# A scanned attention and a feed-forward block on one core: new tables of order, engines, banks and filler products

## The chip, the cores and the metric

The kernel runs on one core of one Trainium2 chip. The metric is the device time of one execution in microseconds. Before the change it is 268.63 us, the median of three runs (267.58 to 268.67).

## The reference

Inputs `r, k, v, w, a, b` are float32 of shape (4, 8, 768, 40): batch, heads, positions, head size. Every head carries a 40 by 40 state through the 768 positions; the rows that it gives are then put through a feed-forward block of 3072 tokens, 320 to 2048 to 320, with a squared ReLU.

```
for t in range(S):
    y[:, :, t] = einsum('bhd,bhde->bhe', rt, state)
    Sa = einsum('bhde,bhe->bhd', state, at)
    state = state * wt[:, :, None, :] - einsum('bhd,bhe->bhde', Sa, bt)
    state = state + einsum('bhd,bhe->bhde', vt, kt)
h = x @ w_in;  r = maximum(h, 0);  out = (r * r) @ w_out
```

## The kernel before, in words

The scan over 768 positions is cut into 6 chunks of 128 positions. A *batch* m (24 of them) is one chunk of one of the four inputs' batches, all 8 heads; a *step* st (48) is half a batch, four heads. Each batch is prepared (`add_prep`), each step goes through the products that solve the recurrence inside a chunk (`add_step`), and when both steps of a batch are done its 128 tokens go into the feed-forward block (`add_ff`, 14 groups h, of one batch for the first four and of two after them).

Preparation of a batch: six loads of 160 KB (`NW`, `NK`, `NB`, `NA`, `NV`, `NR`, L293), all issued from SyncE (SP); the logarithm of w on ScalarE (`lnW`, L307); sums over positions on TensorE (L317, L321, L328) into a bank; exponentials on ScalarE (`GI`, `GA`, L352); a copy of `GA` shifted by one position, `E`, by two small transfers from SP (L362; the first three batches compute it, L332); the products `KB` (L383) and `AA` (L389) and the casts `RV` (L246); then transposes, on TensorE with a copy out of the bank (`AT`, `KBT`, `RVT`, L399 with L243 or L246), or from batch 10, 16 and 20 on by a transposing transfer from SP (L426).

A step: 8 products L522 into two banks, two masked copies on VectorE (`CN`, L530), products `P` (L539, L545), a copy `Mc`, correction L554, difference `c` (L567), correction again, a copy `SN`, a transpose and copy `TB`, 8 products L608, two masked copies on VectorE (`EVX`, L613), products y (L628 to L646), then `Xn` (L652) and `UZ` (L659). `x` (L571) and `Cc` (L575) feed a sum that guards the result.

Feed-forward: transposes of `Xn` (L765) to `XT`, products with the 320 by 2048 weights `WIN` (L790 for the last 64 rows, L803 for the others), ReLU `hs` (L810 on ScalarE, L812 on VectorE), square `Gt` (L819, L821), products with `WOUT` (L837), copy `osb` and a store (L845). `WIN` and `WOUT` are loaded by transfers that GpSimd (POOL) issues (L727, L730, L739).

Nothing here is ordered by a scheduler at run time. Each operation is registered by `op(...)` with the engines that could do it; `placed()` then reads four tables that are written out in the code. `ORDER` is one list of all 2135 operations: each engine executes its own in the order of that list, and waits there for what it needs, with everything behind it on that engine waiting too. `WAYS` picks the engine of the operations that have a choice (VectorE, ScalarE, GpSimd). `BANKS` picks one of the eight accumulator banks for each group of products. `IDLE` puts so many products of ones, whose result nobody reads (L1010), ahead of a TensorE operation. A bank, or a buffer of a ring, that is still in use holds up its next writer.

Of the kernel before, what the change touches and what calls it, by code (L numbers as in the profile page):

```python
# [18 lines left out]
def kernel(  # L19
# [14 lines left out]
    NB, NHH, T, D = r.shape  # L34
    L = 128
# [227 lines left out]
    for m in range(NBC):  # L263
        o = Batch()
# [613 lines left out]
    def add_guard():  # L878
# [32 lines left out]
        "!,!3#C!!#I!(!&!$!+!6!-#L!7!<!?!=!@!O!8!9!>$@!P!4!F!A!;$F!S!D!*!E!I!V#J#K!W!K!J!L!Q#E!T!U"  # L911
        "!:!R!o!B!Z#M!G!2#D#F!H!q!p$I!#!r$G![!]#Q!M$K#R!^$H!d!_#N#S!X!`%;!N#O%A!a!b!c!Y!s#X$J!5%B"
        "%C$C#G$A#Y$D$B&:)6$E!t!.#T#V#W$L$M#q!u#P#]#_&~!C%D%F!v!w#s#^#r#H!{!|%E!g!}$O$P$N!e!/!f#!"
        "#`%<%=#t$S$U!~$R!h#u#v&@$T&A!i!x#a#b$Q##$V((!y!j&B&C#c#d$Y#w#x!k#%#$#U$[&D#y#e#f$Z$n#(#)"
        "$p#Z%K$]#}!l#[$^#i&E$_!1#.()%I!m#~!%$!#g$o#&!n%L#z#j$#$`$$(*%J#k#l#/#0$W#1%H%>$w$X$c&H$q"
        "$r%R%G$s$a!z#{&I$%&<#h%S$&&G&;&=)<#5$t#2#3#8$u$+#m$v#6%M#n#<$z#o$(!0$b&F%?%P$f%Q#|$x(!#4"
        "$d#=%@$,$-#7(+$e&J%k(#$g&K$y&>!)#p)z&L$.(&${#9(%%m#:%l)=%t#;%V%X$|$h%W&?$i(,%N$/&Q$2$~$}"
        ")>(-%Y$0&O%n&R%!%Z%O%[(0$j%#%%$k%T%]$l$m%$($%o&P(.(/%p%`%q(1$1%U)?&U%r%s%^$5%w&V&W)@#>%x"
        "$3%_(3(2%u&M(9%&(:)A&j$4&N%(%a&k&l%y%c$6)D&X&m$9%z(6$7*#(5%d&n+2+v&s$:$8&_)E%{%e%)&Y&o%*"
        "(4%-(7&p%g%+&q&r&Z#,#*%f*$#+%.+8(8%|&S&T&v%~&[%}(=(>(?*%#-(;&])8(Q(S%v%0%4%h(<&^%b*&&w(@"  # L920
        "&t+9&u)7&x)9)B)C):(A%j(R%i)|);*(*)(F(T(B$;$<&`(C(D*,&a&z){*-%1&b(U(V)G&$(G&c+|(E(H#?(Z%2"
        "&d(W(X(I&!&y+:([&e(J)}&{&|(h*++4(Y#@)F&f&%-.&#**&&(K#A&g(^(L(M(_)M)H&h&i%,+;+=+<+}+5)~)K"
# [12 lines left out]
        "10/C11+*/V0%2x/W)1/o.=1.2{1$++/X*b.>121m+,/p1/2z/`,l.?,t,{,x.Q,u/@.R.S,y,s/A.9,|,}/Y/E.@"
# [42 lines left out]
    IDLE = ((132, 1, 1), (38, 21, 4), (60, 4, 5), (135, 2, 5), (62, 1, 5), (223, 11, 7), (168, 1, 5), (89, 3, 4), (230, 11, 7), (232, 6, 6), (239, 5, 7), (241, 2, 5), (109, 1, 0))  # L978
# [140 lines left out]
```

## Time and profile before

| | before |
|---|---|
| span of the profiled execution | 267.4 us |
| runs | 268.67, 267.58, 268.63 us |
| TensorE busy (matmul) | 247.5 us, 93% |
| VectorE (DVE) busy | 236.8 us, 89% |
| ScalarE (ACT) busy | 205.0 us, 77% |
| GpSimd (POOL) busy | 176.7 us, 66% |
| HBM | 123 GB/s over the span |

The profile has no time of its own for the execution beside the span of 267.4 us from the first to the last instruction; the median of the runs is 1.2 us above that span. Busy TensorE time is not TensorE at its peak, since matmuls overlap and their ends are modelled.

### The profile page before, as it was taken

The numbers are of one execution on the slowest core, as the hardware profiler recorded it, in microseconds if no ns is written. First come the engines' busy times: TensorE is split into PE (matmuls) and PEld (weight loads), VectorE is DVE, ScalarE is ACT, GpSimd is POOL, SyncE is SP. The second block draws the span as 40 slices with busy tenths as digits, with TensorE's granted clock in tenths as the row PEclk, the third lists the DMA queues.
The fourth block names the chain that finished last, engine by engine and source line by source line (L and its number), as shares of the span: only waits on it lengthen the run. The fifth ranks groups of instructions, "written<-read, shape, count | busy, mean of one in ns | idle before, by whom it ended". The sixth has DMA issues, their size and how long they took to land.

```text
span 267.4 us, 10182 instructions
## 1 busy us (share of the span) xinstructions
PE 247.5 (93%) x3972; PEld 194.3 (73%) x3972; DVE 236.8 (89%) x559; ACT 205.0 (77%) x549; POOL 176.7 (66%) x289
## 2 busy tenths in 40 slices
PE   7888599999999999999989999999999998799993
PEld 6566487777788687778768688777777786577772
DVE  4799969998999989999999998998999997787681
ACT  3577659897668999687888879898969898477640
POOL 3559559769749999975684747974865754356220
PEclk9999979999999999999999999999999999999998
DMA  7999989899899579899897389997898888771202
GB/s 125 186 166 150 208 164 161 148 175 170 161 171 167 109 137 205 125 166 175 169 190 141 83 165 177 162 150 156 168 165 159 160 171 164 155 182 21 75 2 77
DMA packets 184553, 39.86 MB, mean 149 GB/s; under 512 B 176331, under 2 KB 184118, under 8 KB 184502
## 3 DMA queue, kind: packets, MB, share of 16 engines
q1 hardware_dynamic: 181942, 36.56, 76.6%
q0 software_dynamic: 2560, 2.62, 6.1%
q8 instruction: 31, 0.51, 0.8%
q14 instruction: 20, 0.16, 0.2%
HBM read 28.84 MB, written 3.93 MB: 123 GB/s over the span
## 4 chain that ended last, share of the span: by engine, by line
PE 50%; DMA 14%; DVE 14%; SPq 7%; ACT 5%; POOL 5%; issue 4%; DVEq 0%; POOLq 0%; ACTq 0%
PE bank L837 14%; PE bank L803 10%; SPq L293 6%; DVE CN L530 4%; PE bank L790 4%; DVE EVX L613 3%; DMA WOUT<-in_moe_w_out_dram 3%; PE bank L522 3%; DMA WIN<-in_moe_w_in_dram 3%; PE bank L608 3%; PE bank L399 3%; PE bank L554 3%; PE bank L628 2%; DMA KBT<-KB 2%; PE bank L321 2%
## 5 line engine op out<-in xcount | busy, mean ns | idle before, releaser
L613 DVE TENSOR_TENSOR EVX<-bank,MEX 128x512 bf16<-128x512 f32 x96 | 62.6, 682 | 2.4 <-PE bank L608 1.4
L530 DVE TENSOR_TENSOR CN<-bank,MCN 128x512 bf16<-128x512 f32 x96 | 61.7, 680 | 3.4 <-PE bank L522 2.9
L837 PE MATMUL bank<-WOUT,Gt 128*128 128x320 bf16 x384 | 59.1, 299 | 1.6 <-DMA WOUT<-in_moe_w_out_dram 0.5
L803 PE MATMUL bank<-XT,WIN 128*128 128x256 bf16 (+1 forms) x448 | 55.0, 258 | 0.0
L810 ACT ACTIVATE hs<-bank 128x512 bf16<-128x512 f32 x74 | 43.0, 598 | 12.1 <-PE bank L803 5.5
L837 PEld LDWEIGHTS <-Gt 128*128 128x128 bf16 x384 | 35.2, 97 | 14.6 <-issue 1.6
L821 POOL TENSOR_TENSOR Gt<-hs 128x512 bf16<-128x512 bf16 x35 | 36.2, 1042 | 14.1 <-DVE hs L812 12.1
L803 PEld LDWEIGHTS <-WIN 128*128 128x128 bf16 x448 | 34.7, 98 | 5.5 <-issue 0.6
L579 ACT ACTIVATE junk<-CN 128x512 bf16<-128x512 bf16 x48 | 30.2, 630 | 1.0 <-DVE CN L530 0.5
L571 POOL TENSOR_TENSOR x<-Mc,c 128x160 f32<-128x160 bf16 x40 | 19.9, 502 | 15.0 <-DVE Cc L575 9.1
L819 ACT ACTIVATE Gt<-hs 128x512 bf16<-128x512 bf16 x39 | 24.5, 631 | 5.2 <-DVE hs L812 5.0
L575 POOL TENSOR_TENSOR Cc<-x,SN 128x160 bf16<-128x160 f32 x41 | 21.6, 526 | 3.8 <-ACT SN L243 1.8
L389 POOL TENSOR_TENSOR AA<-NA,E 128x320 bf16<-128x320 f32 (+1 forms) x20 | 15.7, 783 | 12.4 <-DMA E<-GA 6.1
L383 POOL TENSOR_TENSOR KB<-NK,GI 128x320 bf16<-128x320 f32 (+1 forms) x22 | 18.7, 852 | 7.2 <-DMA NK<-in_k_dram 3.6
L554 PEld LDWEIGHTS <-CN 128*128 128x128 bf16 x384 | 18.8, 97 | 6.4 <-issue 3.5
L383 POOL TENSOR_TENSOR KB<-NB,GI 128x320 bf16<-128x320 f32 (+1 forms) x21 | 18.4, 875 | 6.7 <-ACT hs L810 3.4
L335 POOL TENSOR_TENSOR r<-lnW 128x320 f32<-128x320 f32 x18 | 13.1, 728 | 12.3 <-ACT lnW L307 6.2
L243 ACT ACTIVATE TB<-bank 128x512 bf16<-128x512 bf16 (+1 forms) x32 | 17.4, 548 | 4.5 <-PE bank L595 3.2
L522 PE MATMUL bank<-AT,KBT 64*128 64x128 bf16 x384 | 18.5, 217 | 2.1 <-DMA AT<-AA 0.8
L790 PE MATMUL bank<-XT,WIN 64*128 64x256 bf16 (+1 forms) x224 | 18.5, 259 | 1.9 <-DMA WIN<-in_moe_w_in_dram 1.9
L812 DVE TENSOR_SCALAR hs<-bank 128x512 bf16<-128x512 f32 x22 | 14.8, 684 | 4.5 <-PE bank L803 3.4
L608 PE MATMUL bank<-RVT 64*128 64x128 bf16 x192 | 15.3, 219 | 2.3 <-ACT hs L810 1.3
(128 smaller groups left out, 656.8 us busy)
## 6 DMA issues: line engine op xcount, KB each, us to landing
NW<-in_w_dram SPq DMA_DIRECT2D x24, 160.0 KB, 3.6
NK<-in_k_dram SPq DMA_DIRECT2D x24, 160.0 KB, 3.8
NB<-in_b_dram SPq DMA_DIRECT2D x24, 160.0 KB, 3.7
NA<-in_a_dram SPq DMA_DIRECT2D x24, 160.0 KB, 3.9
NR<-in_r_dram SPq DMA_DIRECT2D x24, 160.0 KB, 3.7
NV<-in_v_dram SPq DMA_DIRECT2D x24, 160.0 KB, 3.7
out_dram<-osb SPq DMA_DIRECT2D x24, 160.0 KB, 2.4
E<-GA SPq DMA_DIRECT2D x21, 112.0 KB, 3.3
```

The source lines that it names most:

```text
L383: engine(eng).tensor_tensor(out=o.KB.tile[:, u, h, 0:D], in0=o.nat[key].tile[:, h], op=ALU.mult, in1=o.GI.tile[:, h])
L522: nc.tensor.matmul(out=quads(ca[s])[:, i, u, :], lhsT=o.KBT.tile[half(s), u, j0 + i, :], rhs=o.AT.tile[half(s), j0 + i, :], start=(i == 0 ...
L530: nc.vector.tensor_tensor(out=t_[:, :, s], in0=quads(ca[s]), in1=MCN[:], op=ALU.mult)
L554: nc.tensor.matmul(out=P[:, 2 * i + s], lhsT=CN[:, i, s, 1, :], rhs=X[:, 2 * i + s], start=False, stop=last, skip_group_check=True)
L579: nc.scalar.activation(out=t_, in_=CN_.tile[:, :, :, 1, :], func=ACTF.Square, accum_out=ACC[:, AN + st:AN + st + 1])
L613: nc.vector.tensor_tensor(out=sb(EV_, [128, 2, 2, 2, L], BF16)[:, :, s], in0=quads(ex[s]), op=ALU.mult, in1=MEX[:].rearrange("p (i u) x -> ...
L790: nc.tensor.matmul(out=hv(w_)[:, u], lhsT=WIN[2][half(w_), j * 128:(j + 1) * 128], rhs=XT()[half(w_), 2, 0:nb, :], start=(u == 0), stop=False,
L803: nc.tensor.matmul(out=hv(w_)[:, u], lhsT=WIN[g][:, (j0 + u) * 128:(j0 + u + 1) * 128], rhs=XT()[:, g, 0:nb, :], start=False, stop=(g == 1 ...
L810: nc.scalar.activation(out=t_, in_=hpb.tile[:], func=ACTF.Relu)
L819: nc.scalar.activation(out=t_, in_=x_, func=ACTF.Square)
L821: engine(eng).tensor_tensor(out=t_, in0=x_, in1=x_, op=ALU.mult)
L837: nc.tensor.matmul(out=opb.tile[:, 0:DM], lhsT=Gtb[h].tile[:, j, b_, :], rhs=WOUT[:, j, :], start=(j == 0), stop=(j == NJ - 1))
```

## The change

Only the four tables are new. The operations, their sizes, the tiles, the rings and the loads are the same.

- `ORDER`: nearly every operation stands elsewhere. 
- `WAYS`: 21 operations leave GpSimd; 14 of them go to VectorE and 7 to ScalarE, net. Counted by kind, before to after, on VectorE: `SN` 6 to 21, `x` 8 to 14, `TB` 16 to 22, `Cc` 7 to 12, `AA` 5 to 9, `lo` 1 to 4, `KB` 7 to 9, `AT` 11 to 13; `Mc` 19 to 11, `hs` 22 to 15, copy of `Xn` 12 to 8, `RVT` 10 to 8, `KBT` 7 to 5, casts `RV` 5 to 3, `Gt` 22 to 21, `r` 3 to 2, `XT` 8 to 7, `osb` 10 to 9. On GpSimd: `KB` 43 to 41, `Cc` 41 to 36, `x` 40 to 34, `Gt` 35 to 36, casts 31 to 24, `AA` 20 to 16, `lo` 20 to 17, `r` 18 to 19, copy of `Xn` 12 to 16. On ScalarE: `hs` 74 to 81, casts 14 to 23, `Mc` 29 to 37, `SN` 42 to 27, `TB` 32 to 26, `RVT` 7 to 9, `KBT` 4 to 6, `AT` 10 to 8.
- `BANKS`: another bank for most groups of products.
- `IDLE`: 69 products of ones become 76; before they end ahead of the first feed-forward group, now ahead of step 6's second correction.
- Of TensorE's L837 products, 72 stand behind the last L628 product in the old order, 64 in the new.

```
@@ placed()'s tables; two lines of each long one @@
     ORDER = (
-        "!,!3#C!!#I!(!&!$!+!6!-#L!7!<!?!=!@!O!8!9!>$@!P!4!F!A!;$F!S!D!*!E!I!V#J#K!W!K!J!L!Q#E!T!U"
+        "!6!9!8!3!7!+!4#C!,!!!(!<!5$@!=!?!;!>!F!@!&!#!I!:!%!Q!J!P!T!O!D!U#F!V!E!K!W#I!2#E!o!L!p$F"
...
     WAYS = (
-        "0012201001001111100011001100021202001100011110000110000100100020100001010000001000001100"
+        "0011210111121110111110000100001202000000221110001010010000202020100000201100111010011000"
...
     BANKS = (
-        "0123456725743652745274532031645073610376154731576135372650613724567143726073062173671532"
+        "0123456702345672301427401324713610276732450632046401304620176347201732154603712645135207"
...
-    IDLE = ((132, 1, 1), (38, 21, 4), (60, 4, 5), (135, 2, 5), (62, 1, 5), (223, 11, 7), (168, 1, 5), (89, 3, 4), (230, 11, 7), (232, 6, 6), (239, 5, 7), (241, 2, 5), (109, 1, 0))
+    IDLE = ((26, 5, 6), (38, 9, 6), (49, 7, 0), (51, 4, 0), (82, 6, 4), (89, 19, 2), (148, 13, 3), (155, 6, 6), (349, 4, 1), (331, 6, 3),)
```

The code that reads them, unchanged:

```
        for o, x in zip([o for o in row if o.alts], WAYS, strict=True):
            o.eng, o.cost, o.lat = o.alts[int(x)]
        at = [DIGITS.index(a) * 91 + DIGITS.index(b) for a, b in zip(ORDER[::2], ORDER[1::2], strict=True)]
        for i, n, bank_ in IDLE:
            row[i].idle = n, bank_
```

First place: SyncE at the start of the program, the first loads. `NW_176` before and `NW_165` after are batch 0's w; `NW_167` before and `NW_176` after are batch 1's. Before:

```order
L293 DMA NW_167<-in_w_dram 128x8x40
L293 DMA NW_176<-in_w_dram 128x8x40
L293 DMA NK_181<-in_k_dram 128x8x40
L293 DMA NB_190<-in_b_dram 128x8x40
L293 DMA NA_192<-in_a_dram 128x8x40
L293 DMA NW_195<-in_w_dram 128x8x40
```

After:

```order
L293 DMA NW_165<-in_w_dram 128x8x40
L293 DMA NA_167<-in_a_dram 128x8x40
L293 DMA NB_169<-in_b_dram 128x8x40
L293 DMA NK_172<-in_k_dram 128x8x40
L293 DMA NW_176<-in_w_dram 128x8x40
L293 DMA NW_184<-in_w_dram 128x8x40
```

Batch 0's w moved from second to first, its a from fifth to second; batch 1's w from first to fifth.

Second place: GpSimd around the issue of the first feed-forward weights. Before:

```order
L383 TENSOR_TENSOR KB_91<-NK_368,GI_187 128x8x40
L571 TENSOR_TENSOR x_470<-Mc_313,c_340 128x160
L203 MEMSET SN_110 128x4x24
L575 TENSOR_TENSOR Cc_473<-x_470,SN_107 128x160
L246 CAST RV_104<-NR_378 128x8x40
L571 TENSOR_TENSOR x_561<-Mc_313,c_418 128x160
L339 TENSOR_TENSOR lo_362<-r_360 128x320
L727 DMA WIN_116<-in_moe_w_in_dram 128x2048
L730 DMA WIN_117<-in_moe_w_in_dram 64x1024 x2
L383 TENSOR_TENSOR KB_92<-NK_481,GI_275 128x8x40
L203 MEMSET SN_112 128x4x24
L246 COPY Xn_589<-Xn_589 128x64
```

After:

```order
L383 TENSOR_TENSOR KB_91<-NK_373,GI_197 128x8x40
L383 TENSOR_TENSOR KB_91<-NB_409,GI_197 128x8x40
L730 DMA WIN_117<-in_moe_w_in_dram 64x1024 x2
L246 CAST RV_104<-NV_457 128x8x40
L727 DMA WIN_115<-in_moe_w_in_dram 128x2048
L727 DMA WIN_116<-in_moe_w_in_dram 128x2048
L383 TENSOR_TENSOR KB_92<-NK_502,GI_325 128x8x40
```

The weights stand right behind batch 2's `KB`, where five elementwise operations and a memset stood between; the last piece, `WIN_115`, stood four operations further on and now stands with the others. On TensorE, 353 matmuls stood ahead of the first product that reads `WIN` (L790), and 425 do now.

Third place: VectorE at the last batch's `AA`, which waits for the last `E` transfer. Before:

```order
L530 TENSOR_TENSOR CN_297<-bank_84,MCN 128x2x256
L821 TENSOR_TENSOR Gt_1052<-hs_810 128x512
L613 TENSOR_TENSOR EVX_475<-bank_82,MEX 128x2x256
L389 TENSOR_TENSOR AA_101<-NA_719,E_99 128x8x40
L246 COPY Xn_1013<-Xn_1013 128x64
```

After:

```order
L613 TENSOR_TENSOR EVX_541<-bank_85,MEX 128x2x256
L383 TENSOR_TENSOR KB_92<-NB_487,GI_325 128x8x40
L652 TENSOR_TENSOR Xn_1026<-bank_84,E_96 128x160
L652 TENSOR_TENSOR Xn_567<-bank_81,E_97 128x160
L246 COPY Xn_1026<-Xn_1026 128x64
L567 TENSOR_TENSOR c_341<-bank_82,Mc_1219 128x160
L652 TENSOR_TENSOR Xn_567<-bank_85,E_97 128x160
L389 TENSOR_TENSOR AA_101<-NA_599,E_99 128x8x40
```

`AA` stood between the two `EVX` of one step; now all four `EVX` of the two steps and six smaller operations stand ahead of it.

124 lines of the change are left out of this document (62 added, 62 removed).

## The prediction

> **What bounds the kernel now.** I read the page first, then the program cut in three by what VectorE (DVE) does: before its first `CN`, up to its last `EVX`, and the rest. The columns of a window are its length, then each engine's busy time, granted clock, DMA share, GB/s.
>
> ```profile
> span 267.4 us, 10182 instructions
> PE 247.5 (93%) x3972; PEld 194.3 (73%) x3972; DVE 236.8 (89%) x559; ACT 205.0 (77%) x549; POOL 176.7 (66%) x289
> ...
> 0.00:11.10 11.10, 8.69 (x80) 6.78 (x80) 5.48 (x23) 5.22 (x13) 4.99 (x17) 1.00 0.91 149
> 11.10:247.55 236.45, 223.19 (x3757) 176.17 (x3755) 220.90 (x510) 192.37 (x521) 168.15 (x268) 0.99 0.89 157
> 247.55:267.40 19.85, 15.59 (x146) 11.37 (x142) 10.45 (x28) 7.38 (x16) 3.61 (x6) 0.94 0.14 52
> ```
>
> In the long middle TensorE and VectorE are both near full: VectorE is busy 220.90 of 236.45 us. So the middle cannot shrink by better hops alone. It can shrink only where VectorE idles (236.45 - 220.90 = 15.55 us), where its instructions take longer than they need, or where work leaves it. I therefore make the sum on VectorE: start, middle, tail. Two stretches carry much of the idle time:
>
> ```profile
> 28.00:37.00 9.00, 6.44 (x108) 5.19 (x104) 6.73 (x20) 4.02 (x14) 3.71 (x8) 0.81 0.98 190
> 221.00:233.00 12.00, 9.72 (x147) 7.44 (x144) 8.66 (x20) 7.62 (x19) 4.63 (x9) 1.00 0.79 156
> ```
>
> ```profile
> PE bank L790 <- DMA WIN<-in_moe_w_in_dram: 1.9, 2, 1.5
> DVE AA L389 <- DMA E<-GA: 1.8, 1, 1.8
> PE bank L522 <- DMA AT<-AA: 0.8, 1, 0.8
> ```
>
> VectorE idles 9.00 - 6.73 = 2.27 us in the first and 12.00 - 8.66 = 3.34 us in the second, 5.6 together. The waits (who waited for what: total, times, longest) name the cause: the feed-forward weights land late in the first, the last `E` and a transposed `AA` in the second. All three are transfers that stood too close to their reader.
>
> **Start.** These are ScalarE's and VectorE's rows (start, length, instruction, idle time before and what ended it):
>
> ```profile
> 3.86 0.47 ACT L307 ACTIVATE lnW<-NW 128x320 f32<-128x320 f32 x1 [1.54 <-DMA NW<-in_w_dram]
> 5.09 0.47 ACT L307 ACTIVATE lnW<-NW 128x320 f32<-128x320 f32 x1 [0.76 <-DMA NW<-in_w_dram]
> ...
> 7.55 0.91 DVE L205 MEMSET UZ<- 128x1024 uint32 x1 [0.16 <-issue]
> 8.38 0.26 DVE L389 TENSOR_TENSOR AA<-NA,E 128x160 bf16<-128x160 f32 x1
> ```
>
> Batch 0's logarithm is the second, at 5.09; with its w loaded first it takes the first's place, 1.23 us earlier. The first `AA` stood behind a memset of 0.91 us, which now runs before any load has landed, so up to 2.1 us could be won at the first `CN`. Against it, batch 0's k is now the fourth load and not the third, and a place in the queue is worth about as much as the two logarithms are apart; and what stands on VectorE up to step 3 is more work than before. Ends 0 and -2.1; I take **-1.5 us**, nearer the logarithms' own rows.
>
> **Work that moves to VectorE.** Mean durations are the figure behind "busy us,":
>
> ```profile
> L248 DVE TENSOR_SCALAR SN<-bank 128x160 bf16<-128x160 f32 x6 | 1.8, 319 | 0.3 <-PE bank L554 0.3
> L571 DVE TENSOR_TENSOR x<-Mc,c 128x160 f32<-128x160 bf16 x8 | 4.3, 539 | 0.0
> L246 DVE COPY TB<-bank 128x512 bf16<-128x512 bf16 (+1 forms) x16 | 6.5, 407 | 0.1
> L575 DVE TENSOR_TENSOR Cc<-x,SN 128x160 bf16<-128x160 f32 x7 | 3.3, 473 | 0.0
> L389 DVE TENSOR_TENSOR AA<-NA,E 128x320 bf16<-128x320 f32 (+1 forms) x5 | 2.7, 533 | 1.8 <-DMA E<-GA 1.8
> L339 DVE TENSOR_TENSOR lo<-r 128x320 bf16<-128x320 f32 x1 | 0.7, 731 | 0.0
> ...
> L812 DVE TENSOR_SCALAR hs<-bank 128x512 bf16<-128x512 f32 x22 | 14.8, 684 | 4.5 <-PE bank L803 3.4 <-ACT Gt L819 0.8
> L246 DVE CAST Mc<-bank 128x160 bf16<-128x160 f32 x19 | 5.9, 315 | 0.4 <-PE bank L545 0.4
> L246 DVE COPY Xn<-Xn 128x64 bf16<-128x64 bf16 x12 | 4.3, 362 | 0.1
> L246 DVE COPY RVT<-bank 128x1024 bf16<-128x1024 bf16 (+1 forms) x10 | 6.5, 653 | 0.0
> ```
>
> Added: 15 `SN` 4.8, 6 `x` 3.2, 6 `TB` 2.4, 5 `Cc` 2.4, 4 `AA` 2.1, 3 `lo` 2.2, and 4 of `KB` and `AT` at about `AA`'s 0.53, 2.1: 19.2 us. Removed: 7 `hs` 4.8, 8 `Mc` 2.5, 4 `Xn` copies 1.4, 2 `RVT` 1.3, and eight others (two `KBT`, two casts, one each of `Gt`, `r`, `XT` and `osb`) at 0.56, between these rows, 4.5: 14.5 us. **+4.7 us** of VectorE time. VectorE is busy 93% of the middle, so nothing hides it; I carry it whole. ScalarE gets 7 `hs` and 9 casts for fewer `SN` and `TB`; with 192.37 of 236.45 us busy in the middle it has room, and I cost this at nothing. Were its cover gone, seven operations of about 0.6 us would be 4 us.
>
> **TensorE.**
>
> ```profile
> L1010 PE MATMUL bank<-ones_b 128*128 128x128 bf16 x69 | 6.1, 221 | 0.1
> ```
>
> Seven more products of ones at 6.1/69 = 0.09 us are 0.6 us, and they stand in the first third, where TensorE waits anyway (2.56 us idle in 28 to 37 alone). Nothing on the sum; 0.6 if that cover is gone.
>
> **Idle time recovered.** The sizes and landings of the transfers (KB each, median us to landing):
>
> ```profile
> E<-GA SPq DMA_DIRECT2D x21, 112.0 KB, 3.3
> ...
> WIN<-in_moe_w_in_dram POOLq DMA_DIRECT2D x2, 512.0 KB, 8.0
> ```
>
> ```profile
> L613 DVE TENSOR_TENSOR EVX<-bank,MEX 128x512 bf16<-128x512 f32 x96 | 62.6, 682 | 2.4 <-PE bank L608 1.4 <-ACT junk L714 0.5
> L821 DVE TENSOR_TENSOR Gt<-hs 128x512 bf16<-128x512 bf16 x22 | 12.4, 565 | 0.1
> L571 POOL TENSOR_TENSOR x<-Mc,c 128x160 f32<-128x160 bf16 x40 | 19.9, 502 | 15.0 <-DVE Cc L575 9.1 <-DVE c L567 4.4 <-DVE GL L375 1.3
> ```
>
> The weights move ahead of five GpSimd operations, `x`, `Cc`, a cast, `x` and `lo`, some 2.5 us at the 0.50 of GpSimd's `x` (last row), the last piece by four more, and 72 more matmuls stand ahead of the first reader. Eight microseconds of landing then end before the reader comes: I expect that wait of 1.9 us gone. The last `AA` gets three `EVX` and six small operations ahead of it; the `EVX` alone are 3 x 0.68 = 2.0 us, against the 1.8 us that it waited. Of the 5.6 us in the two holes I take 4.6 back. Of the other 15.55 - 5.6 = 9.9 us, spread over the middle at under 5%, I take 2: counted in `ORDER`, at least 40 TensorE matmuls now stand between the place of any `E` transfer and its first reader, median 108, where ten of the 42 had fewer (two of them none) and the median was 74; for the weights the smallest count goes from 63 to 157. **-6.6 us**; ends 0 (each gap is filled by another late operand) and -12.
>
> **Waits inside VectorE's instructions.** These are minimum, median and maximum durations of single kinds on VectorE:
>
> ```profile
> L571 DVE TENSOR_TENSOR x<-Mc,c x8: 308/460/869, 60.1 to 233.7; 128x160 f32<-128x160 bf16 x8
> L575 DVE TENSOR_TENSOR Cc<-x,SN x7: 310/318/999, 32.5 to 250.1; 128x160 bf16<-128x160 f32 x7
> L821 DVE TENSOR_TENSOR Gt<-hs x22: 411/423/930, 47.5 to 259.6; 128x512 bf16<-128x512 bf16 x22
> L246 DVE COPY Xn<-Xn x12: 171/237/1042, 36.4 to 248.9; 128x64 bf16<-128x64 bf16 x12
> L652 DVE TENSOR_TENSOR Xn<-bank,E x48: 307/315/326, 25.2 to 248.7; 128x160 bf16<-128x160 f32 x48
> ```
>
> The same instruction takes 308 or 869 ns, with no wait outside it. Against the minimum, 8 `x` lose 8 x 0.23 = 1.8, 7 `Cc` 7 x 0.16 = 1.1, 12 copies 12 x 0.19 = 2.3, and 22 `Gt`, whose mean is 565, 22 x 0.15 = 3.4: 8.6 us over 49 instructions, 0.18 each. All of them read and write SBUF alone, as GpSimd's do; the last row, a product that reads a bank, stays between 307 and 326. GpSimd loses 21 operations. If the tables place these instructions where GpSimd is between two of its own, up to 8.6 us could go; if they meet more often, it grows. I take **-2.5 us**, in the lower half because the number of exposed instructions rises. Ends -8.6 and +8.
>
> The Trainium skill, SBUF — State Buffer, section "Who interferes with whom", says that VectorE and GpSimd share one pair of ports as an exclusive lock, also for a two-input VectorE operation with both inputs in SBUF, and that the later one blocks until the other is done. The maxima above agree: 869 is 308 and about one GpSimd operation. By that rule moving work from GpSimd to VectorE buys little where the two run together; a whole block for each of the 20 moved two-input operations is the slower rival below.
>
> **Tail.**
>
> ```profile
> 247.88 1.25 PE L837 MATMUL bank<-WOUT,Gt 128*128 128x320 bf16 x8
> 248.96 0.33 PE L765 MATMUL bank<-IDb,Xn 128*128 128x128 bf16 x3
> ```
>
> Eight L837 products move from behind the last y to ahead of it, where TensorE has gaps. They held TensorE from 247.88 to 248.96: **-1.1 us**. The rest of the tail has the same pieces. End 0, if `Xn` is then late instead.
>
> **Sum.** 267.4 - 1.5 + 4.7 - 6.6 - 2.5 - 1.1 = 260.4 us of span; the median of the runs is 1.2 above the span of before (268.63 against 267.4), which gives **261.6 us**.
>
> **Rivals.**
> 1. *VectorE blocked by GpSimd: slower.* `x`, `Cc`, `AA`, `lo` and `KB` on VectorE rise by 20. If each loses what the worst rows lose (869 - 308 and 999 - 310, about 0.6) and not the 0.2 in its mean, that is 20 x 0.4 = 8 us instead of the 2.5 gained: 260.4 + 10.5 = 270.9 of span, 272.1. It decides against before once the exposed instructions lose 7.0 us more than I take, 0.13 us for each of some 55. For it: the rows above. Against: GpSimd has less to do. 0.13.
> 2. *No change.* The holes close, but VectorE's idle time comes back in front of `CN` and `EVX`: 3 of 15.55 us recovered, no port wait saved: 267.4 - 1.5 + 4.7 - 3.0 - 1.1 = 266.5, 267.7. For it: both engines are near full, so a late operand anywhere costs. 0.13.
> 3. *Twice the gain.* Idle time falls by 12 and port waits by 6: 267.4 - 1.5 + 4.7 - 12 - 6 - 1.1 = 251.5, 252.7. For it: if order and durations agree, VectorE can run at over 98%. Against: no stretch of before does over 10 us. 0.14.
> 4. *The clock halves more often.* In 28 to 37 us the granted clock was 0.81, so about 3.4 us ran at half and 1.7 were lost. The filler products that stood there are gone. Two more such stretches: 261.6 + 3.4 = 265.0. 0.06. The Trainium skill, TensorE: Matmul & The Clock Gate, section "What's actually happening", has the clock halved after an idle window of some 3.4 us; the 0.81 agrees with one such window.
>
> The forecast itself has 0.54, with its own range 257 to 266.
>
> **Chances and range.** A measurement of this kernel can tell about 0.5% from no change, 1.3 us: 267.3 to 270.0. Faster: nearly all of the forecast 0.53, rival 3 0.14, rival 4 0.05, some of rival 2 0.05, 0.77. Slower: rival 1 less its lower end 0.11, a little of rival 2, 0.13. Same: 0.10. The range reaches from 253.5, between rival 3 and the forecast, to 269.5, which leaves out most of rival 1 above and half of rival 3 below.
>
> **What would show it.** Start: the first `CN` on VectorE at 9 to 10 us, not 11.1. Weights: no wait of L790 for `WIN`, and a clock of 1.00 from 25 to 40 us. VectorE: busy over 95% between first `CN` and last `EVX`, and a middle of 229 to 233 us. Port waits: medians of `x` and `Gt` near 310 and 410 ns. Tail: under 19 us after the last `EVX`. The forecast is wrong if VectorE's busy time in the middle grows by over 7 us, or if its idle time there stays above 12 us.

## The result, and the profile after

The changed kernel takes 266.29 us (median of 11 runs, 263.08 to 268.62), the kernel before 268.94 us in the same rounds (11 runs, 267.06 to 271.84). The ratio is 0.987, with a 95% interval of 0.983 to 0.991: 1.3% faster, about 3.5 us where 7 were forecast. The ratio leaves out runs in a slower state (for the changed kernel 4 of 11, the profiled one at 267.04 us among them, by a narrow margin), while the medians of all runs differ by 2.65 us, 1.0%. Two more measurements on other chips gave 0.985 (0.975 to 0.996) and 0.990 (0.985 to 0.994).

The page of the changed kernel, first lines (span, then busy time, share and instructions of each engine):

```profile
span 265.6 us, 10167 instructions
PE 248.5 (94%) x3982; PEld 195.9 (74%) x3982; DVE 233.5 (88%) x573; ACT 207.9 (78%) x556; POOL 163.7 (62%) x268
```

The changed program, cut as in the prediction at VectorE's first `CN` and last `EVX` (length, busy time of TensorE, its weight loads, VectorE, ScalarE, GpSimd, granted clock, DMA share, GB/s):

```profile
0.00:9.85 9.85, 7.98 (x75) 6.56 (x75) 6.57 (x23) 4.49 (x10) 3.78 (x18) 1.00 0.90 147
9.85:247.20 237.35, 225.94 (x3775) 178.70 (x3776) 218.07 (x526) 195.86 (x529) 156.02 (x245) 0.99 0.89 157
247.20:265.60 18.40, 14.54 (x139) 10.62 (x135) 8.84 (x25) 7.54 (x19) 3.86 (x6) 1.00 0.15 56
```

Start and tail came as forecast: 11.10 to 9.85 us and 19.85 to 18.40. The middle did not: 236.45 became 237.35 us. VectorE's busy time there fell by 2.8 us (220.90 to 218.07), and its idle time grew by 3.7 (15.55 to 19.28). What VectorE saved, it waited. Two more profiles of the changed kernel, on other chips (spans 268.8 and 266.2 us), say the same: between their own cuts VectorE is busy for 219.3 and 218.6 us and idle for 21.9 and 19.1.

When it waits is seen in three stretches, of before first and then of the changed kernel (same columns):

```profile
0.00:60.00 60.00, 51.10 (x847) 40.42 (x847) 50.78 (x131) 42.70 (x115) 39.65 (x80) 0.97 0.98 165
60.00:210.00 150.00, 145.73 (x2445) 115.29 (x2446) 144.67 (x335) 126.22 (x344) 113.51 (x175) 1.00 0.91 158
210.00:250.00 40.00, 37.50 (x573) 29.16 (x570) 33.16 (x76) 29.91 (x78) 21.51 (x35) 1.00 0.64 132
```

```profile
0.00:60.00 60.00, 53.62 (x884) 43.63 (x885) 52.51 (x138) 45.45 (x125) 35.65 (x72) 0.94 1.00 167
60.00:210.00 150.00, 146.62 (x2468) 117.11 (x2468) 140.26 (x340) 128.95 (x348) 106.28 (x163) 1.00 0.88 155
210.00:250.00 40.00, 36.49 (x538) 26.69 (x538) 33.18 (x77) 28.64 (x75) 19.70 (x31) 1.00 0.71 142
```

Between 60 and 210 us, where VectorE idled for 5.33 of 150 us, it now idles for 9.74 (10.74 and 10.31 in the other two profiles). In this pair TensorE idles less up to 60 us (8.9 to 6.4) and more from 210 to 250 (2.5 to 3.5). The two holes that the prediction named are mostly closed, and no product waits for `WIN` any more:

```profile
28.00:37.00 9.00, 7.65 (x104) 5.39 (x103) 7.85 (x22) 6.68 (x18) 3.78 (x9) 0.64 0.97 182
221.00:233.00 12.00, 11.78 (x174) 8.42 (x171) 10.70 (x25) 6.92 (x16) 7.77 (x13) 1.00 0.81 152
```

VectorE's idle time in them went from 5.6 to 2.45 us (9.00 - 7.85 and 12.00 - 10.70). Its waits in the changed kernel (who waited for what: total, times, longest):

```profile
DVE CN L530 <- PE bank L522: 3.4, 5, 2.0
DVE hs L812 <- PE bank L803: 3.3, 6, 1.2
DVE c L567 <- PE bank L554: 2.3, 4, 0.8
DVE hs L812 <- POOL Gt L821: 2.1, 2, 1.2
```

Most of it is waiting for TensorE. Summed over VectorE's waits between the cuts, TensorE ended 8.8 us of them before the change and 13.6 after it; transfers ended 1.8 and 0.5. The growth is largest ahead of the difference `c`, less ahead of `CN`, and there is none ahead of `EVX`. Their rows (busy us, mean ns, idle time before them and what ended it), before and then after; the row of `EVX` before stands in the prediction:

```profile
L530 DVE TENSOR_TENSOR CN<-bank,MCN 128x512 bf16<-128x512 f32 x96 | 61.7, 680 | 3.4 <-PE bank L522 2.9 <-ACT GI L352 0.3
L567 DVE TENSOR_TENSOR c<-bank,Mc 128x160 bf16<-128x160 f32 x48 | 15.0, 316 | 0.7 <-POOL RV L246 0.3 <-DVE c L567 0.2
```
```profile
L613 DVE TENSOR_TENSOR EVX<-bank,MEX 128x512 bf16<-128x512 f32 x96 | 62.6, 679 | 2.1 <-PE bank L608 1.5 <-ACT SN L243 0.2
L530 DVE TENSOR_TENSOR CN<-bank,MCN 128x512 bf16<-128x512 f32 x96 | 61.5, 680 | 4.3 <-PE bank L522 3.4 <-ACT junk L579 0.5
L567 DVE TENSOR_TENSOR c<-bank,Mc 128x160 bf16<-128x160 f32 x48 | 14.4, 314 | 3.5 <-PE bank L554 2.3 <-POOL x L571 0.4 <-PE bank L539 0.3
```

TensorE in turn waits late in the program for a transfer that it did not wait for before, the transposed `RVT` (1.2 us in three waits beside its weight loads):

```profile
PE bank L608 <- DMA RVT<-RV: 1.2, 3, 0.5
PE bank L522 <- DMA AT<-AA: 0.7, 1, 0.7
```

### The profile page after: what moved, and what is told of

Read it like the earlier page. It is cut to its first block, busy times and chain, and to the rows that moved or that the text cites. A ratio compares the mean times of both kernels' runs of the same rounds, so it can differ in the third digit from the quotient of the medians.

```text
span 265.6 us, 10167 instructions
## 1 busy us (share of the span) xinstructions
PE 248.5 (94%) x3982; PEld 195.9 (74%) x3982; DVE 233.5 (88%) x573; ACT 207.9 (78%) x556; POOL 163.7 (62%) x268
## 4 chain that ended last, share of the span: by engine, by line
PE 53%; DVE 14%; DMA 11%; ACT 7%; SPq 7%; issue 4%; POOL 2%; DVEq 0%; ACTq 0%
PE bank L837 14%; PE bank L803 10%; SPq L293 5%; DVE CN L530 4%; PE bank L790 3%; DMA RVT<-RV 3%; PE bank L522 3%; PE bank L608 3%; PE bank L399 3%; DVE EVX L613 2%; PE bank L628 2%; PE bank L554 2%; PE bank L321 2%; DMA E<-GA 2%; DMA NW<-in_w_dram 2%
## 5 line engine op out<-in xcount | busy, mean ns | idle before, releaser
L837 PE MATMUL bank<-WOUT,Gt 128*128 128x320 bf16 x384 | 59.0, 299 | 0.7 <-DVE EVX L613 0.6
L810 ACT ACTIVATE hs<-bank 128x512 bf16<-128x512 f32 x81 | 47.0, 599 | 11.9 <-PE bank L803 6.3
L821 POOL TENSOR_TENSOR Gt<-hs 128x512 bf16<-128x512 bf16 x36 | 37.3, 1043 | 27.9 <-ACT hs L810 17.1
L837 PEld LDWEIGHTS <-Gt 128*128 128x128 bf16 x384 | 35.5, 98 | 13.6 <-issue 1.0
L571 POOL TENSOR_TENSOR x<-Mc,c 128x160 f32<-128x160 bf16 x34 | 16.5, 489 | 11.9 <-DVE c L567 8.1
L243 ACT ACTIVATE TB<-bank 128x512 bf16<-128x512 bf16 (+1 forms) x26 | 14.5, 558 | 7.3 <-PE bank L590 2.8
L790 PE MATMUL bank<-XT,WIN 64*128 64x256 bf16 (+1 forms) x224 | 18.7, 259 | 0.7 <-DVE XT L246 0.2
L522 PE MATMUL bank<-AT,KBT 64*128 64x128 bf16 x384 | 17.7, 217 | 1.8 <-DVE KBT L246 0.7
L383 POOL TENSOR_TENSOR KB<-NB,GI 128x320 bf16<-128x320 f32 (+1 forms) x19 | 16.6, 875 | 3.9 <-DMA NB<-in_b_dram 2.2
L628 PE MATMUL bank<-KB,EVX 128*128 128x40 bf16 x384 | 17.4, 181 | 0.9 <-DVE EVX L613 0.9
L575 POOL TENSOR_TENSOR Cc<-x,SN 128x160 bf16<-128x160 f32 x36 | 17.9, 500 | 0.2
L567 DVE TENSOR_TENSOR c<-bank,Mc 128x160 bf16<-128x160 f32 x48 | 14.4, 314 | 3.5 <-PE bank L554 2.3
L628 PEld LDWEIGHTS <-EVX 128*128 128x128 bf16 x384 | 14.7, 97 | 3.7 <-DVE EVX L613 2.5
```

Of the source, the lines that this page charges most:

```text
L383: engine(eng).tensor_tensor(out=o.KB.tile[:, u, h, 0:D], in0=o.nat[key].tile[:, h], op=ALU.mult, in1=o.GI.tile[:, h])
L522: nc.tensor.matmul(out=quads(ca[s])[:, i, u, :], lhsT=o.KBT.tile[half(s), u, j0 + i, :], rhs=o.AT.tile[half(s), j0 + i, :], start=(i == 0 ...
L628: nc.tensor.matmul(out=Y[:, 2 * i + s], lhsT=EV_.tile[:, i, s, u, :], rhs=o.KB.tile[:, u, head(i, s), 0:D], start=first, stop=(u == 1 and ...
L790: nc.tensor.matmul(out=hv(w_)[:, u], lhsT=WIN[2][half(w_), j * 128:(j + 1) * 128], rhs=XT()[half(w_), 2, 0:nb, :], start=(u == 0), stop=False,
L810: nc.scalar.activation(out=t_, in_=hpb.tile[:], func=ACTF.Relu)
L821: engine(eng).tensor_tensor(out=t_, in0=x_, in1=x_, op=ALU.mult)
```

## The experiments

Three readings compete. **Theory B**, the prediction's: VectorE sets the middle, a microsecond of its work is a microsecond of time. **Theory A**: TensorE sets it. **Theory C**: neither alone does; several resources are near full and hand the path to and fro. Beside them stand two narrower questions, whether half clock and whether the transfers ate the gain. All ratios are to the kernel before, run beside each kernel; chips differ (before took 268.94 us in the first set and 271.0 to 272.0 in the others), so ratios are what is compared. One percent is 2.7 us.

### VectorE or TensorE: work added

```diff
+            if s == 1:      # behind each step's second EVX, 48 times
+                nc.vector.tensor_copy(out=probe[:], in_=ex[s].tile[:, 0:160])
```
```diff
+            for _ in range(4):      # ahead of each P, 48 times
+                nc.tensor.matmul(out=Pb.tile[:, 384:512], lhsT=ones_b[:], rhs=ones_b[:], ...)
```

On the changed kernel, VectorE:

> The changed kernel with one more VectorE copy of 128x160 from a bank to SBUF behind the second EVX of each step, 48 in all, read by nobody; nothing is left out. Like the other small bank reads of VectorE they last about 0.31 us, so at most 15 us of VectorE work. Theory A (TensorE's own products, in their written order, now set the middle, and VectorE's 19 us of idle time there are cover): the time grows by clearly less than half of what is added, 3 to 6 us. Theory B (the prediction's: VectorE sets the middle): it grows by nearly all of it, 11 to 15 us. Theory C (the two engines hand the path to and fro inside every step, neither alone sets it): more than half, 8 to 11 us, here and with added TensorE work as well.

Measured 1.006 (1.001 to 1.010). Against the changed kernel's 0.987 that is +1.9%, 5 us, which is Theory A's 3 to 6.

On the changed kernel, TensorE:

> The changed kernel with four more products of ones (128 columns) ahead of every product P, in its own bank, 48 x 4 = 192 in all; nothing is left out. At some 0.055 us each from start to start they are 10.7 us of TensorE work. Theory A (TensorE sets the middle): 9 to 11 us more. Theory B (VectorE sets it): 1 to 4 us more, the rest falls into TensorE's waits. Theory C (the path goes to and fro): 6 to 9 us more.

Measured 1.004 (0.999 to 1.008): +1.7%, 4.5 us, under Theory A's 9 to 11 and Theory C's 6 to 9, and a little above Theory B's 1 to 4. No theory fits both runs.

On the kernel before, VectorE:

> The kernel before with the same 48 VectorE copies, at most 15 us of VectorE work; nothing is left out. Theory A (TensorE sets the middle in both kernels): 3 to 6 us more. Theory B (VectorE set it): 11 to 15 us more. Theory C: 8 to 11. If the bound moved from VectorE to TensorE with the change, this one grows by 11 or more where the changed kernel grows by less than 6.

Measured 1.002 (0.997 to 1.007): 0.5 us, with 0 inside the interval. No theory had so little.

On the kernel before, TensorE:

> The kernel before with the same 192 products of ones, 10.7 us of TensorE work; nothing is left out. Theory A (TensorE sets the middle in both kernels): 9 to 11 us more. Theory B (VectorE set it): 1 to 4. Theory C: 6 to 9. If the bound moved from VectorE to TensorE with the change, this one grows by less than 4 where the changed kernel grows by 9 or more.

Measured 1.007 (1.002 to 1.011): 1.9 us of 10.7. That is Theory B's 1 to 4, but Theory B has just failed the run with VectorE work.

The busy lines of the kernel before with the copies, and with the products:

```profile
PE 251.1 (92%) x3972; PEld 196.8 (72%) x3972; DVE 243.8 (89%) x607; ACT 205.4 (75%) x549; POOL 176.8 (65%) x289
```
```profile
PE 255.2 (94%) x4164; PEld 204.6 (75%) x4164; DVE 236.9 (87%) x559; ACT 205.2 (76%) x549; POOL 176.7 (65%) x289
```

VectorE's busy time rose by 7.0 us (236.8 to 243.8) and the time by 0.5; TensorE's by 7.7 (247.5 to 255.2) and the time by 1.9. In the kernel before, neither engine's work is the path of the middle. In the changed kernel the same additions cost 5 and 4.5 us: the new order leaves less slack on both engines.

The copies also show why the busy time grows by less than their durations. The groups of VectorE instructions, the row of the copies in the kernel before (busy us, mean ns), and a piece of the timeline of the changed kernel with copies (start, length):

```profile
L617 DVE CAST probe<-bank 128x160 bf16<-128x160 f32 x48 | 15.0, 313 | 0.0
```
```profile
99.92 0.32 DVE L568 TENSOR_TENSOR c<-bank,Mc 128x160 bf16<-128x160 f32 x1
100.14 0.32 DVE L249 TENSOR_SCALAR SN<-bank 128x160 bf16<-128x160 f32 x1
100.38 0.68 DVE L247 COPY RVT<-bank 128x1024 bf16<-128x1024 bf16 x1
100.97 0.68 DVE L614 TENSOR_TENSOR EVX<-bank,MEX 128x512 bf16<-128x512 f32 x1
```

The `SN` starts 0.22 us after a `c` that lasts 0.32. Neighbours overlap by some 0.09 us, so a small instruction on a full VectorE adds less than its 0.31 us: the 48 copies added 7.0 and 9.7 us of busy time in the two kernels, 0.15 and 0.20 us each.

### VectorE or TensorE: work taken away

Adding work tells of slack; the change took time away. So this was measured on the kernel before too.

```diff
-                        nc.vector.tensor_scalar(out=t_, in0=hpb.tile[:], ...)
+                        n = 64 if 2 <= h <= 12 else 512
+                        nc.vector.tensor_scalar(out=t_[:, 0:n], in0=hpb.tile[:, 0:n], ...)
...
+                        if eng == "DVE" and 6 <= h <= 12:
+                            t_, x_ = t_[:, 0:1, 0:1, 0:64], x_[:, 0:1, 0:1, 0:64]
                         engine(eng).tensor_tensor(out=t_, in0=x_, in1=x_, op=ALU.mult)
```

> The kernel before with VectorE work taken away in the middle: its 15 hs of feed-forward groups 2 to 12 write 64 of 512 columns, its 12 Gt of groups 6 to 12 square 64 of 512 columns. This leaves out most of those ReLUs and squares, so the feed-forward rows are not computed; the order, the engines and every wait are unchanged. At 684 and 565 ns each before and some 150 to 200 ns narrowed, 15 x 0.5 + 12 x 0.4 = 12 us of VectorE work go. Theory B (the prediction's ledger: VectorE sets the middle): 9 to 12 us faster. Theory F (TensorE's own products, in order, and the landing of transfers set it; VectorE time that is saved turns into waiting): under 3 us faster.

Measured 0.996 (0.992 to 0.999): 1.2 us faster. Its busy line, and its middle cut at its own first `CN` and last `EVX`:

```profile
PE 245.5 (92%) x3972; PEld 194.0 (73%) x3972; DVE 228.8 (86%) x559; ACT 204.7 (77%) x549; POOL 175.4 (66%) x289
```
```profile
11.20:246.50 235.30, 221.70 (x3757) 176.18 (x3755) 213.76 (x510) 192.15 (x521) 167.29 (x269) 0.99 0.89 158
```

VectorE's busy time fell by 8.0 us (236.8 to 228.8; 15 `hs` and 13 `Gt` were narrowed). In the middle it fell by 7.1 and the middle by 1.15; VectorE's idle time there rose from 15.55 to 21.54. This is the prediction's ledger put to the test: of each microsecond of VectorE time that is saved, about 0.15 reaches the end. Theory B is out, for the kernel before.

```diff
+                if h <= 12:
+                    js = [j for j in js if j not in (1, 5, 9)]
                 for j in js:
                     nc.tensor.matmul(out=opb.tile[:, 0:DM], lhsT=Gtb[h].tile[:, j, b_, :], ...)
```

> The kernel before with TensorE work taken away in the middle: 3 of the 16 products with WOUT of each batch but the last two are left out (66 of 384), so the feed-forward rows are not the sums asked for; nothing else changes. At 1.09 us for 8 they are 66 x 0.136 = 9.0 us. Theory B (VectorE sets the middle): under 3 us faster. Theory F (TensorE's products set it, together with transfers): 4 to 9 us faster, the lower end if the transfers' landing takes over at once.

Measured 0.991 (0.988 to 0.994): 2.5 us of 9.0, just inside Theory B's under 3 and short of Theory F's 4 to 9. The row of these products fell from 59.1 to 50.1 us of busy time; TensorE's whole busy time fell by 4.2 us only (247.5 to 243.3), in a profile whose granted clock was 0.973 and not 0.989. TensorE is nearer the path than VectorE, and does not set it either: Theory A is out as well. The waits of this run between 178 and 190 us show where some of it went:

```profile
POOL KB L383 <- DVE CN L530: 3.5, 1, 3.5
DVE CN L530 <- PE bank L522: 2.9, 1, 2.9
PE bank L522 <- DMA KBT<-KB: 2.4, 1, 2.4
```

A piece of `KB` on GpSimd waits for a `CN` on VectorE, its transposing transfer is late, TensorE waits 2.4 us for that, and VectorE 2.9 us for TensorE. Each resource waits for the next one in turn. ScalarE and GpSimd, 77% and 66% busy before the change, were not priced in this way.

### The transfers

The page's chain of waits of the kernel before, by engine, pointed this way, and the prediction did not read it. Below it stands that of the changed kernel:

```profile
PE 50%; DMA 14%; DVE 14%; SPq 7%; ACT 5%; POOL 5%; issue 4%; DVEq 0%; POOLq 0%; ACTq 0%
```
```profile
PE 53%; DVE 14%; DMA 11%; ACT 7%; SPq 7%; issue 4%; POOL 2%; DVEq 0%; ACTq 0%
```

Before the change VectorE has 14% of the chain, no more than the transfers, which with SyncE's queue have 21%. Extra transfers of 512 KB that nobody reads price them:

```diff
+                if g == 0:      # early: ahead of the first weights
+                    nc.gpsimd.dma_start(out=probe[:], in_=moe_w_in[0:128, :])
...
+            if st in (14, 20, 28):      # middle: three of them, behind x
+                nc.gpsimd.dma_start(out=probe[:], in_=moe_w_in[0:128, :])
```

The changed kernel again, as the measure for the three that follow:

> The changed kernel once more, nothing altered, on the chip and in the rounds of the three runs beside it, so that these are measured against it. Ratio to before 0.983 to 0.991, as first measured.

Measured 0.985, 268.60 us.

> The changed kernel with one more transfer of 512 KB, read by nobody, issued from GpSimd right ahead of the first feed-forward weights (about 24 us); nothing is left out. Theory D (the DMA engines are full up to about 40 us, 0.9 and more in every window, and transfers, not engines or clock, set when that stretch ends): step 6's first CN, at 40.7 us, moves by about 512 KB at 170 to 190 GB/s, 2.7 to 3.0 us, and the end by 2 to 3 us. Theory N (TensorE's and VectorE's own work sets that stretch): under 0.7 us at either place.

Measured 0.994 (0.990 to 0.999), 270.23 us: 1.6 us more by the medians and 2.5 by the ratios, whose intervals overlap; so it is not told apart from Theory D's 2 to 3, nor clearly from nothing. The delay does not show at the place expected: the CN meant, at 40.7 us in the changed kernel's first profile, is the 13th of VectorE's 96 (it belongs to step 7, which stands ahead of step 6), and it starts at 41.2 us here and at 41.3 in the run beside it. The loads show it: two that are issued at 25 and 26 us, an `NA` and an `NW`, land after 13.2 and 13.1 us, where they took 9.4 to 10.8 in three profiles of the changed kernel.

> The changed kernel with three more transfers of 512 KB, read by nobody, issued from GpSimd at about 90, 117 and 150 us, where the DMA engines are 0.88 busy; nothing is left out. Theory D2 (the DMA engines set the middle too): 1.5 MB at 155 GB/s are 10 us, of which 5 to 10 us show at the end. Theory A or C (engines and their hops set the middle, loads run ahead): under 1.5 us.

Measured 1.019 (1.009 to 1.029), 275.86 us: 7.3 us more than the run beside it by the medians and 9 by the ratios, from four runs of each; clear of noise, but not to the microsecond. That is Theory D2's side. The chain of waits shows a load right behind the first extra transfer:

```profile
90.31 7.33 DMA NW<-in_w_dram
97.67 0.48 ACT lnW L308
...
104.59 3.29 DMA NW<-in_w_dram
```

Between 85 and 200 us no load of 160 KB takes over 5.3 us to land in three profiles of the changed kernel; here ten take 5.5 to 7.4.

> The kernel before with the same three transfers of 512 KB in the middle that cost the changed kernel about 7 us (275.86 against 268.6 beside it); nothing is left out. If the loads' landing was as near the path before as after (a third resource without slack, beside TensorE and VectorE): 5 to 9 us more. If the new order brought the loads closer to their readers: under 3 us more.

Measured 1.011 (1.005 to 1.017): 3.3 us on the kernel before by the medians, 3.0 by the ratio, at the upper edge of the lower expectation. Loads land close to their readers there too (up to 8.1 us in the same stretch, where 5.6 was the longest), but with more room than after the change.

So the DMA engines, 0.89 busy in the middle of both kernels, are a third resource near the path, and the changed kernel leans on them harder.

### The start

```diff
-        "!6!9!8!3!7!+!4#C!,!!!(!<!5$@!=!?!;!>!F!@!&!#!I!:!%!Q!J!P!T!O!D!U#F!V!E!K!W#I!2#E!o!L!p$F"
+        "#C!6!9!8!3!7!+!4!,!!!(!<!5$@!=!?!;!>!F!@!&!#!I!:!%!Q!J!P!T!O!D!U#F!V!E!K!W#I!2#E!o!L!p$F"
```

> The changed kernel with batch 1's w loaded ahead of batch 0's, as before the change; nothing is left out. The first CN then comes about 1.0 to 1.3 us later (10.9 to 11.2 us). The prediction carried the start's gain whole to the end: 1.0 to 1.3 us slower. Theory D (transfers set when the stretch up to 40 us ends): the delay is gone by step 6's first CN at 40.7 us, and the time is within 0.5 us of the changed kernel's.

Measured 0.987 (0.983 to 0.991) beside 0.985: no difference that can be told. `CN` of this run and of the changed kernel beside it (minimum, median, maximum ns; first and last start):

```profile
L530 DVE TENSOR_TENSOR CN<-bank,MCN x96: 673/681/693, 10.6 to 242.5; 128x512 bf16<-128x512 f32 x96
```
```profile
L530 DVE TENSOR_TENSOR CN<-bank,MCN x96: 673/681/693, 9.2 to 241.5; 128x512 bf16<-128x512 f32 x96
```

The first `CN` is 1.4 us later than in the run beside it, but only 0.7 and 0.5 us later than in the two other profiles of the changed kernel (9.9 and 10.1 us), and earlier than the 10.9 to 11.2 expected. The 13th is at 41.5 against 41.3 us beside it, and 40.7 and 39.0 in the other two. The time and this pair go with Theory D, by which the earlier start is lost by 40 us; but a loss of 1.25 us, 0.5%, could hide in these intervals, so that is not settled, nor that transfers are what absorbs it.

### Half clock

The changed kernel's profiled run has 6.8 us at half clock (30 to 40 us: 0.66), the kernel before 3.4 (0.83). Its runs go by the clock: 264.2 us at a mean of 1.000, 266.1 to 267.1 at 0.987, 268.6 at 0.979. That speaks for the prediction's fourth rival. Fillers, the products of ones of `IDLE`, test it. By the table and by the trace the changed kernel has 79 of them, ten more than before, not 76.

```diff
-    IDLE = ((26, 5, 6), (38, 9, 6), (49, 7, 0), (51, 4, 0), (82, 6, 4), (89, 19, 2), ...)
+    IDLE = ()
```

> The changed kernel without its 76 products of ones; nothing of the computation is left out. Theory H (half clock costs): more half-clock episodes in the first 50 us, mean granted clock 0.96 to 0.98, 268 to 272 us. Theory N (the early stretch waits for operands whatever the clock): within 1 us of the changed kernel.

Measured 1.007 (1.004 to 1.011), clock 0.96 to 0.99: 2.0% slower than the changed kernel, 5.5 us. Theory H.

The opposite, 78 more fillers in the table:

> The changed kernel with 78 more products of ones between about 20 and 37 us, ahead of products that wait there, so that TensorE's array is busier in the stretch where the granted clock fell to half (6.8 us in the changed kernel's profiled run, 0.66 mean in 30 to 40 us); nothing is left out. Theory H (half-clock episodes took back part of the gain, about 1.2 us for each 3.4 us of them): mean granted clock 0.995 or more and 263 to 265 us, 1 to 3 us below the changed kernel. Theory N (the stretch waits for operands whatever the clock): clock higher, time within 0.7 us of the changed kernel's or, as fillers delay what stands behind them, up to 3 us above.

Measured 0.995 (0.991 to 0.998), clock 0.989 to 1.000: 2 us slower than the changed kernel with nearly all half clock gone. The 78 products start 0.056 us apart, 4.4 us in all, and went into a stretch (20 to 40 us) where TensorE was idle for 3.2 us and here still is for 2.5; so most of them pushed other products back. Whether it was through their banks was not shown. The next set is smaller and stands behind `P`, in unused columns of its own bank:

```diff
+            for _ in range({3: 5, 4: 9, 5: 6}.get(st, 0)):      # behind P, in P's own bank
+                nc.tensor.matmul(out=Pb.tile[:, 384:512], lhsT=ones_b[:], rhs=ones_b[:], start=False, ...)
```

> The changed kernel once more, nothing altered, as the measure for the two runs with fillers beside it. Ratio to before 0.983 to 0.991.

Measured 0.990, 267.97 us.

> The changed kernel with 20 more products of ones: 5, 9 and 6 behind the products P of steps 3, 4 and 5, in unused columns of P's own bank, where TensorE's next product waits 0.4 to 0.8 us for a bank that VectorE still reads; so they delay nothing, unlike the 78 of the earlier run, which went into banks that others waited for. Nothing is left out. Theory H (half clock between 30 and 38 us costs 2 to 3 us when it comes; filled without delaying anything, that is won): clock 1.00 from 25 to 40 us, step 6's first CN 2 us earlier, time 1.5 to 2.5 us under the changed kernel. Theory N (that stretch ends when VectorE and the transfers are done, whatever the clock): clock full, time within 0.7 us.

Measured 0.988 (0.983 to 0.993), 268.15 us: the same as the changed kernel. The stretch from 30 to 40 us, of the changed kernel and of this one:

```profile
30.00:40.00 10.00, 9.43 (x139) 7.17 (x136) 7.47 (x23) 7.45 (x20) 2.67 (x5) 0.66 0.91 167
```
```profile
30.00:40.00 10.00, 8.68 (x170) 6.82 (x168) 8.96 (x27) 8.95 (x26) 3.70 (x8) 1.00 0.95 175
```

The clock is full and more gets done: 170 products instead of 139, and the 13th `CN` starts at 39.8 and not 40.7 us. The end does not move. The unaltered kernel beside it happened to have full clock there as well, had its 13th `CN` at 39.0, 1.7 us ahead of the first profile, and of that lead 0.4 us was left at the 85th, at 209.3 us.

With 28 more late in the program (`IDLE` entries ahead of three products and five behind step 43's P):

> The run with 20 more products of ones and, beside these, 28 between 213 and 235 us, where several profiles of the changed kernel show another half-clock stretch of 3.4 us (mean clock 0.83 in 210 to 220 us). Nothing is left out. Theory H: mean granted clock 0.995 or more, 2 to 4 us under the changed kernel. Theory N: within 1 us of it.

Measured 0.994 (0.991 to 0.997), clock 0.991 to 1.000: 1.2 us slower than the unaltered kernel beside it, at the edge of noise. Theory H fails both times, and Theory N holds within that. Removing fillers costs, adding more does not pay: the present ones are enough. Why runs with a lower clock are slower is not settled; a late transfer can lengthen the time and, by leaving TensorE idle, lower the clock as well. The run with the early transfer has such a place: behind 57.7 us, after a wait for a load in which TensorE was busy for 1.7 of 3.4 us, its clock is halved for 6.8 us.

### The order alone, the engines alone

> The changed kernel's order, banks and fillers with the engines of before (tables ORDER, BANKS and IDLE new, WAYS old); nothing is left out. The prediction's ledger gives the order the recovered idle time, the start and the tail (9.2 us together) and the engines +4.7 of VectorE work and -2.5 of port waits: the order alone would be the faster half, 259 to 262 us. Theory A (TensorE sets the middle; order and engines were chosen as one): the new order with the old engines has late operands in other places, and is no faster than before, 268 to 274 us.

Measured 1.071 (1.064 to 1.079), 291.6 us. VectorE's row for `EVX` in that run (busy, mean ns, idle time before it and what ended it):

```profile
L613 DVE TENSOR_TENSOR EVX<-bank,MEX 128x512 bf16<-128x512 f32 x96 | 63.3, 681 | 14.7 <-PE bank L608 14.7
```

> The kernel before with the changed kernel's engines alone (WAYS new, ORDER, BANKS and IDLE old); nothing is left out. The prediction's ledger: +4.7 of VectorE work less 2.5 of port waits, 270 to 272 us. Theory A (TensorE sets the middle; order and engines were chosen as one): operands late in other places, 270 to 276 us, with VectorE's idle time and TensorE's waits both larger than before. If the gain came from the engines, it is 266 to 267 us.

Measured 1.135 (1.126 to 1.145), 308.2 us. Both are far worse than any expectation. The order is made for the engines: `WAYS` differs for 278 of its 720 operations (the 21 that leave GpSimd are a net count), and with these on the engines of before `EVX` waits 14.7 us where it waited 2.4 before the change and 2.1 after it. The change's parts cannot be added up, as the prediction added them.

No run is faster than the changed kernel by more than can be measured.

## Why the prediction was wrong

**The step that failed** is the one ahead of all terms: "I therefore make the sum on VectorE". Two engines were near full and the prediction put the whole ledger on one. The run with VectorE work taken away shows what that ledger is worth in the kernel before: 8.0 us of busy time less, 1.2 us of time. The term in which it shows is *Idle recovered*: -6.6 us were forecast, and VectorE's idle time in the middle grew by 3.7 (3.5 and 6.4 in the two other profiles).

The Trainium skill, Perfetto Trace Analysis, section "Identifying the Most-Contended Engine", names the engine with the highest occupancy as the one to optimize first, and judges TensorE by other measures than its busy share. By that VectorE, 93% busy in the middle, comes first, as in the prediction; here a microsecond taken from it gave 0.15 us, and one taken from TensorE, 94% busy, gave 0.28, so occupancy did not name the path. The Trainium skill, Perfetto Trace Analysis, section "Optimization Strategy", says to find the gaps on that engine and what blocks it there; the prediction's own rows name TensorE for 3.4 of the 4.5 us ahead of `hs` and 1.4 of the 2.4 ahead of `EVX`, and it went after the waits for transfers.

**By its terms:**

- *Start, -1.5:* measured -1.25 at the first `CN` (-1.0 and -1.9 in the two other profiles), right there. But it was carried to the end, and giving it back changed nothing that could be measured.
- *Work moved, +4.7:* a little too large. With kinds and shapes kept apart, the net counts at before's mean durations come to 3.7 us. And it was "carried whole", where even 7.0 us of added VectorE work cost the kernel before 0.5.
- *Port waits, -2.5:* too small. The moved instructions stand in the sum at before's means, waits included; so what they saved is the new count times the fall of the mean: `x` 14 x 0.11, `Cc` 12 x 0.05, `Gt` 21 x 0.10 and copies of `Xn` none, 4.3 us, and 7.0 over all of VectorE's instructions (5.4 and 5.0 in the two other profiles). The rows are below; the medians of `x` and `Gt` are 322 and 416 ns, as said. No run tests by itself that these are waits for GpSimd.
- *Idle recovered, -6.6:* the two holes gave 3.2 of the 4.6 us taken, and the wait for `WIN` is gone. The other idle time, of which 2 us were to go, grew from 9.95 to 16.83. This is where the forecast's missing microseconds are: waits for transfers fell, and waits for TensorE took their place.
- *Tail, -1.1:* -1.45 measured, right (18.4 us in all three profiles of the changed kernel).
- *Fillers, nothing:* counted wrongly, since ten were added and not seven, 0.9 us and not 0.6. What these ten cost was not measured.
- *ScalarE, nothing:* no run prices it. Its share of the chain of waits went from 5% to 7%.

Two of these errors are of opposite sign. VectorE's busy time in the middle was to grow by 2.2 us (4.7 - 2.5) and fell by 2.8, 5 us better than forecast, and its idle time came out 10.3 us worse. That the time lies inside the stated range is luck to that extent, and that VectorE's work fell and the middle did not is the same finding as in the run with work taken away.

```profile
L571 DVE TENSOR_TENSOR x<-Mc,c 128x160 f32<-128x160 bf16 x14 | 6.0, 429 | 0.0
L575 DVE TENSOR_TENSOR Cc<-x,SN 128x160 bf16<-128x160 f32 x12 | 5.0, 420 | 0.0
L821 DVE TENSOR_TENSOR Gt<-hs 128x512 bf16<-128x512 bf16 x21 | 9.5, 463 | 0.7 <-ACT hs L810 0.4 <-PE bank L837 0.2
L246 DVE COPY Xn<-Xn 128x64 bf16<-128x64 bf16 x8 | 2.9, 368 | 0.0
```

**The rivals.** VectorE blocked by GpSimd: no, VectorE's instructions became shorter. No change: its mechanism is in the main the one that happened, idle time coming back, though ahead of `c` (0.7 to 3.5 us), `CN` (3.4 to 4.3) and `hs`, and not ahead of `EVX` (2.4 to 2.1); the measured gain lies between its 0.9 us and the forecast's 7.0. Twice the gain: VectorE was busy for 92% of the middle and not 98%. Half clock more often: it did come, twice as long in the profiled run, but filling it up brought nothing. Of the marks set in advance, "idle time there stays above 12 us" was the one that told: it was 19.28.

**What the gain is** stays open. On VectorE's cuts, start and tail gave 2.7 us between the two profiled runs and the middle took back 0.9. Read on TensorE, idle time gave 2.8 us (267.4 - 247.5 = 19.9 to 265.6 - 248.5 = 17.1) and busy time took back 1.0 of it, which is the span's 1.8; the longer half clock may be a part of the 1.0. But the two other profiles of the changed kernel have 18.9 and 19.6 us of TensorE's idle time, so most of the 2.8 does not hold from one profile to the next. What holds in all three is less idle TensorE up to 60 us (8.9 to 6.4, 7.3 and 7.5) and behind 250 us (4.3 to 3.8 or 3.9), and more from 210 to 250 us (2.5 to between 3.4 and 3.6), where transposed transfers now come late. Which of the many moved operations made the first 60 us denser was not separated; order and engines work only together.

## What to carry to other kernels

Before a sum is made on the engine that looks fullest, ask what a microsecond on it is worth: read its share of the chain of waits, and if a run is to be had, take some of its work away and see what comes out at the end. Where three resources are each near nine tenths busy, saving on one mostly turns into waiting, and the forecast should be a small part of the saving. An order, an engine choice and a set of filler products that were found together are one thing; their parts priced singly do not add up, and alone each may be far worse than neither.

## What the runs showed of the hardware

- Consecutive VectorE instructions overlap in the record by about 0.09 us. 48 copies of 0.313 us (15.0 us in all) raised VectorE's busy time by 7.0 and 9.7 us in the two kernels.
- A half-clock stretch needs no long gap. The stretch ahead of it, 27 to 30 us, still had TensorE busy for 1.91 of 3.00 us, with no gap over 0.73 us between its products; another profile of the same kernel had 1.99 of 3.00 there and no half clock behind it. Half clock in this part of the program came in lengths of 3.4, 6.8 and 10.2 us, beginning between 30.4 and 34.5 us in different runs of nearly the same work. The Trainium skill, TensorE: Matmul & The Clock Gate, section "What's actually happening", has a free-running window of 3.4 us; the lengths, multiples of it, agree with that, and the spread of the beginnings fits, though these kernels differ a little.

```profile
27.00:30.00 3.00, 1.91 (x32) 1.47 (x31) 3.00 (x9) 2.23 (x9) 2.04 (x5) 1.00 1.03 205
```

- In the middle, 512 KB of transfers that nobody reads cost the changed kernel some 2.4 to 3 us each. Beside them single loads of 160 KB took up to 7.3 us to land, where 5.2 was the longest without them, though the DMA engines' mean share was 0.89.
